# Late loads moved from GpSimd's queue to SyncE's, and half of the spectrum weights loaded early, in an S4 convolution with a one-token expert

## Chip, cores, metric

One core of one Trainium2 chip. The time is device microseconds of a whole execution. A profile is one execution, and its span is some 1.8 us shorter than the time that the same execution is given. Runs are marked fast or slow; a run more than 1.5% above the fastest of its kernel counts as slow, one alone can be of unknown state, and comparisons of times use fast runs.

Engine names in the profile: PE is TensorE's matmuls, PEld its weight loads, DVE is VectorE, ACT ScalarE, POOL GpSimd, SPq SyncE's DMA issues. In the code SP, AC, DV, PO are SyncE, ScalarE, VectorE and GpSimd.

## What is computed

`u` is 2048 x 512 in bf16. The output is `x + s * g`:

```python
xn = layernorm(u)
# S4 convolution by FFT: K[d, l] = Re sum_n C * exp(dt*A*l) * dt*B; y = irfft(rfft(xn, 4096) * rfft(K, 4096))
s  = y + xn * Dskip
# mixture of depths, capacity 1: only the token with the largest r = xn @ w_r goes through the expert
r  = xn @ w_r ; i = argmax(r)
e  = (silu(xn[i] @ w_gate) * (xn[i] @ w_up)) @ w_down * sigmoid(r[i])
g  = silu(xn + scatter(e at i))
out = u + s * g
```

## The kernel before

The FFT is done as matmuls in two steps (F1, then F2T). Between them the data take a round trip through DRAM, which reorders them: AT is stored to `scr_a` and read back as BT. The filter's spectrum K2T is a matmul with the 5.2 MB table W. The product PAB of spectrum and signal goes through the first inverse step (FA), as ZT to `scr_z`, back as DD, and through the last step. The channels come in two halves for AT and BT, and in four parts afterwards.

A program in the kernel lists all operations as numbered nodes, finds their dependences by the memory they touch, and issues them on each engine in the order of fixed lists (`_ORDER`). Each engine issues its list in order, DMAs included, so an entry that waits holds up all behind it: GpSimd stood idle for 42.4 us before WD, and the loads of W came right behind it. The parts that matter here:

```python
_FILL = [(12, 6, 1), (15, 5, 1), ...]       # matmuls whose results nobody reads, by place and PSUM bank; 14 in all
_ORDER = {
    "sync": [..., 188, 198, 193, 203, 392, 391, 393, 394, 390,      # AT stores of half 0, BT reads, AT store of half 1
        385, 380, 375, 420, 430, ...],                              # the other three AT stores, then scr_z stores
    "gpsimd": [
        21, 287, 294, 286, 295, 288, 293, 285, 296, 361, 23, 22, 306, 370, 305, 694, 774, 714, 796,],
    # 21 F2T; 285-288 and 293-296 the expert's gate and up; 361 WD; 22, 23, 305, 306 W by quarters; 370 FA; 694.. XR

o_s = cur[0]                                 # these share AT's memory:
AT = place("AT", [128, 32, 256], BF16)       #   stores 375, 380, 385, 390 each free a quarter of it
cur[0] = o_s
K2T = place("K2T", [128, 2, 2, 2, 256], BF16)        # over the quarter of store 375
PAB = place("PAB", [128, 2, 2, 2, 2, 256], BF16)     # its two buffers: over 380 and 385
ZT = [place(f"ZT{i}", [128, 1024], BF16) for i in range(2)]  # over 390
...
W = place("W", [128, 16, 2, 5, 128], BF16)
FA = place("FA", [128, 16, 3, 128], BF16)
XT = place("XT", [128, 2, 2, 4, 128], BF16, o_w + 25600)     # XT, ERU, ERG, WD lie over W's second half and FA
ERU = place("ERU", [128, 4, 1408], BF16, o_w + 30720)
WD = place("WD", [128, 11, 512], BF16, o_w + 41984)
ERG = place("ERG", [128, 4, 1408], BF16, o_w + 41984)

def wload(k):
    if k is None:
        g.dma(PO, [(FA[:], t_fa.ap()...)])
        return
    g.dma(PO, [(W[:, 4 * k:4 * k + 4], t_w.ap()...)])
...
g.dma(PO, [(WD[:, 0:10, :], ...), (WD[0:96, 10, :], ...)])   # after the gate's matmuls: WD lies on ERG
g.dma(PO, [(XRp[:], ...)])                                    # u again, for the last addition
```

W's first half lies on memory that nothing else uses, so its load depends on nothing.

## Time and profile before

| | before |
|---|---|
| time, median of 4 runs | 192.69 us (192.24 to 193.85) |
| span of the profiled execution | 192.6 us (it took 194.4, marked slow) |
| moved by DMA | 37.18 MB |
| first K2T | 89.94 us |

The profiled execution took longer than all four and is marked slow. The first part of the page gives each engine's busy time, its share of the span and the number of instructions; the third part has the DMA queues with packets, MB and share of the engines' time (q1 is SyncE's queue, q0 GpSimd's). The kernel before:

```profile
PE 144.0 (75%) x2280; PEld 106.9 (55%) x2280; DVE 141.3 (73%) x321; ACT 144.8 (75%) x192; POOL 14.1 (7%) x24
...
q1 hardware_dynamic: 39170, 22.51, 43.1%
q0 software_dynamic: 2464, 14.19, 20.2%
```

No engine is above 75%: the time is in waits.

### The profile page before, as it was taken

The numbers are of one execution on the slowest core, as the hardware profiler recorded it, in microseconds if no ns is written. First come the engines' busy times: TensorE is split into PE (matmuls) and PEld (weight loads), VectorE is DVE, ScalarE is ACT, GpSimd is POOL, SyncE is SP. The second block draws the span as 40 slices with busy tenths as digits, with TensorE's granted clock in tenths as the row PEclk, the third lists the DMA queues.
The fourth block names the chain that finished last, engine by engine and source line by source line (L and its number), as shares of the span: only waits on it lengthen the run. The fifth ranks groups of instructions, "written<-read, shape, count | busy, mean of one in ns | idle before, by whom it ended". The sixth has DMA issues, their size and how long they took to land.

```text
span 192.6 us, 5283 instructions
## 1 busy us (share of the span) xinstructions
PE 144.0 (75%) x2280; PEld 106.9 (55%) x2280; DVE 141.3 (73%) x321; ACT 144.8 (75%) x192; POOL 14.1 (7%) x24
## 2 busy tenths in 40 slices
PE   0213579776699799790999999986999999974580
PEld 0001445663479543370997888863899799931120
DVE  2989899998995799661169999689598375282742
ACT  3998688999977986753799999989787995761031
POOL 0018000000003302000000000020002000400000
PEclk9999999999958969798599999999799999996555
DMA  3899920306696999992002279985000469999984
GB/s 91 249 354 387 394 112 5 109 3 198 180 351 192 242 404 412 429 424 88 0 8 53 54 210 275 235 263 119 2 3 3 112 199 257 191 296 286 216 199 111
DMA packets 41946, 37.18 MB, mean 193 GB/s; under 512 B 26977, under 2 KB 37218, under 8 KB 41026
## 3 DMA queue, kind: packets, MB, share of 16 engines
q1 hardware_dynamic: 39170, 22.51, 43.1%
q0 software_dynamic: 2464, 14.19, 20.2%
q8 instruction: 18, 0.29, 0.6%
q10 hardware_dynamic: 288, 0.13, 0.2%
q14 instruction: 6, 0.05, 0.1%
HBM read 26.34 MB, written 10.49 MB: 191 GB/s over the span
## 4 chain that ended last, share of the span: by engine, by line
PE 37%; DMA 23%; DVE 16%; ACT 15%; SPq 4%; issue 2%; DVEq 0%; ACTq 0%
PE PB L187 36%; DMA scr_a<-AT 15%; ACT AT L758 4%; SPq L210 4%; DVE TT L729 4%; ACT XT L975 4%; DVE ST L821 4%; DMA scr_z<-ZT 3%; DVE PAB L729 3%; DMA X<-in_A_u_dram 3%; DMA DD<-scr_z 3%; DVE GG L729 2%; ACT U L758 2%; ACT SC L758 2%; DVE QQ L729 1%
## 5 line engine op out<-in xcount | busy, mean ns | idle before, releaser
L187 PE MATMUL PB<-KT,W 128*128 128x128 bf16 x640 | 44.4, 232 | 6.1 <-ACT K2T L758 4.5
L187 PEld LDWEIGHTS PB<-KT,W 128*128 128x128 bf16 x640 | 40.1, 105 | 9.2 <-ACT K2T L758 5.0
L729 DVE TENSOR_TENSOR PAB<-U,K2T 128x1024 bf16<-128x1024 bf16 x32 | 21.2, 687 | 23.2 <-ACT K2T L758 23.2
L729 DVE TENSOR_TENSOR TT<-GG,ZB 128x512 bf16<-128x512 bf16 (+2 forms) x64 | 28.0, 468 | 0.5
L758 ACT ACTIVATE K2T<-PB 128x1024 bf16<-128x1024 f32 x16 | 16.5, 1034 | 8.2 <-DMA scr_a<-AT 4.5
L187 PE MATMUL PB<-CA,AD 64*128 64x512 bf16 (+1 forms) x64 | 9.7, 381 | 15.0 <-ACT EE L758 7.2
L729 DVE TENSOR_TENSOR QQ<-QQ,EE 128x2048 bf16<-128x2048 bf16 x16 | 19.5, 1218 | 0.1
L758 ACT ACTIVATE ZT<-PB 128x1024 bf16<-128x1024 f32 x16 | 16.5, 1030 | 3.7 <-PE PB L187 3.7
L758 ACT ACTIVATE KT<-PB 128x640 bf16<-128x640 f32 (+1 forms) x24 | 15.6, 648 | 4.6 <-PE PB L187 4.5
L187 PE MATMUL PB<-PAB,FA 64*128 64x128 bf16 x512 | 17.2, 217 | 0.9 <-DVE PAB L729 0.9
L758 ACT ACTIVATE U<-PB 128x1024 bf16<-128x1024 f32 x16 | 15.9, 1021 | 2.4 <-PE PB L187 2.3
L758 ACT ACTIVATE EE<-PB 128x1024 bf16<-128x1024 f32 x16 | 15.9, 1037 | 1.5 <-PE PB L187 1.4
L758 ACT ACTIVATE AT<-PB 128x1024 bf16<-128x1024 f32 x16 | 16.0, 1076 | 1.3 <-PE PB L187 1.3
L187 PE MATMUL PB<-DD,CB 128*128 128x512 bf16 x32 | 11.8, 503 | 6.1 <-DMA DD<-scr_z 5.8
L187 PEld LDWEIGHTS PB<-PAB,FA 64*128 64x128 bf16 x512 | 14.6, 94 | 3.0 <-DVE PAB L729 1.5
L729 DVE TENSOR_TENSOR GG<-TT 128x512 bf16<-128x512 bf16 (+2 forms) x32 | 15.0, 470 | 0.5
L187 PE MATMUL PB<-XN,CB 128*128 128x256 bf16 (+1 forms) x80 | 13.4, 311 | 1.3 <-ACT AT L758 1.3
L729 DVE TENSOR_TENSOR TF<-PB,XN 128x512 bf16<-128x512 f32 x12 | 8.1, 688 | 8.1 <-PE PB L187 8.1
L187 PEld LDWEIGHTS PB<-CA,AD 64*128 64x128 bf16 x64 | 3.5, 116 | 18.1 <-ACT EE L758 8.6
L187 PE MATMUL PB<-BT,F2T 128*64 128x256 bf16 x128 | 11.0, 299 | 2.5 <-ACT U L758 1.6
L187 PE MATMUL PB<-GG,QQ 128*128 128x80 bf16 x256 | 12.1, 200 | 0.6 <-DVE QQ L729 0.3
L187 PEld LDWEIGHTS PB<-GG,QQ 128*128 128x128 bf16 x256 | 10.4, 98 | 2.1 <-ACT KT L758 0.6
(133 smaller groups left out, 227.0 us busy)
## 6 DMA issues: line engine op xcount, KB each, us to landing
W<-c_w POOLq DMA_DIRECT2D x4, 1280.0 KB, 15.0
scr_a<-AT SPq DMA_DIRECT2D x8, 512.0 KB, 4.4
BT<-scr_a SPq DMA_DIRECT2D x8, 512.0 KB, 5.6
scr_z<-ZT SPq DMA_DIRECT2D x16, 256.0 KB, 4.5
DD<-scr_z SPq DMA_DIRECT2D x6, 512.0 KB, 5.8
XR<-in_A_u_dram POOLq DMA_DIRECT2D x4, 512.0 KB, 6.2
out_dram<-XR SPq DMA_DIRECT2D x8, 256.0 KB, 4.7
X<-in_A_u_dram SPq DMA_DIRECT2D x3, 512.0 KB, 6.0
```

The costliest lines, as they stand in the source:

```text
L187: fns.append(lambda e, o=o, l=l, r=r, st=st, sp=sp, tp=tp: e.matmul(o, lhsT=l, rhs=r, start=st, stop=sp, tile_position=tp, skip_group_chec ...
L210: fns.append(lambda e, dst=dst, src=src: e.dma_start(dst, src))
L729: g.V(lambda e: e.tensor_tensor(out=o, in0=a, in1=b, op=op), [o], [a, b], n, mode)
L758: nd = g.A(lambda e: e.activation(out=o, in_=i, func=func, **kw), [o], ins, n + (110 if "bias" in kw or isinstance(kw.get("scale"), bass.A ...
L821: g.V(lambda e, b=b: e.bn_stats(ST[:, b, :], X0[:, b, :]), [ST[:, b, :]], [X0[:, b, :]], 512)
L975: g.A(lambda e, pv=pv, xt=xt: e.activation(out=xt, in_=pv, func=ACT.Copy), [XT[:, bq % 2]], [PB[:, bank, :]], 1024)
```

## The change

Its intent: the two loads of W's first half, which wait for nothing, go out among the expert's weights; all other late loads leave GpSimd for SyncE; and the order lists of all engines are made anew to suit. The diff, with the lists cut to the places that matter:

```diff
-_FILL = [(12, 6, 1), (15, 5, 1), (43, 4, 2), (49, 4, 2), (69, 4, 1), (72, 4, 3), (73, 4, 3), (206, 2, 1)]
+_FILL = [(12, 6, 2), (17, 5, 1), (33, 1, 1), (35, 1, 1), (43, 4, 1), (44, 4, 3), (49, 4, 2), (50, 4, 2), (65, 6, 1),
+         (66, 6, 3), (70, 4, 3), (71, 4, 1), (73, 4, 2), (76, 4, 1), (205, 2, 1)]
 "sync":
-        ... 188, 198, 193, 203, 392, 391, 393, 394, 390, 385, 380, 375, 420, ...
+        ... 193, 188, 198, 375, 203, 394, 392, 391, 361, 380, 393, 390, 305, 370, 306, 385, 512, 509, 420, ...
 "gpsimd":
-        21, 287, 294, 286, 295, 288, 293, 285, 296, 361, 23, 22, 306, 370, 305, 694, 774, 714, 796,
+        21, 285, 23, 295, 286, 287, 22, 288, 293, 294, 296,
 (the lists of ScalarE, VectorE and TensorE are new too: the same nodes in another order;
  left out as well: three names that nothing reads, and the estimated cost of one node)
-                g.dma(PO, [(FA[:], ...)])
+                g.dma(SP, [(FA[:], ...)])
-            g.dma(PO, [(W[:, tsl], ...)])
+            return g.dma(PO if k < 2 else SP, [(W[:, tsl], ...)])
-            g.dma(PO, [(WD[:, 0:10, :], ...
+            g.dma(SP, [(WD[:, 0:10, :], ...
-            g.dma(PO, [(XRp[:], ...)])
+            g.dma(SP, [(XRp[:], ...)])
```

## The prediction

> **What bounds the kernel now.** I read the page's slices first, then the chain of waits, then the DMA view of the stretch that it points at, then the timelines of the engines there. In the page's slices (each 4.8 us), the rows of TensorE, its clock and the DMA:
>
> ```profile
> PE   0213579776699799790999999986999999974580
> PEclk9999999999958969798599999999799999996555
> DMA  3899920306696999992002279985000469999984
> GB/s 91 249 354 387 394 112 5 109 3 198 180 351 192 242 404 412 429 424 88 0 8 53 54 210 275 235 263 119 2 3 3 112 199 257 191 296 286 216 199 111
> ```
>
> Slices 14 to 17 (67 to 87 us) run at 404 to 429 GB/s, all that this trace ever reaches, and TensorE stands still in slice 18 right behind them. Slices 6 and 8 carry 5 and 3 GB/s: there is an idle DMA system 25 to 45 us earlier. The chain of work that ended last says the same; start, length, what:
>
> ```profile
> 59.43 0.58 SPq L210
> ...
> 61.46 28.40 DMA scr_a<-AT
> ...
> 89.94 1.03 ACT K2T L758
> 90.97 0.05 issue
> 91.02 8.60 PE PB L187 x129
> ```
>
> A 512 KB store of AT, half a spectrum buffer, takes 28.4 us to land, and ScalarE's first K2T waits for it, because K2T lies on AT's memory. The DMA view of 57 to 92 us tells why:
>
> ```profile
> DMA packets 5411, 10.88 MB, mean 311 GB/s; under 512 B 199, under 2 KB 4295, under 8 KB 4766
> q0 software_dynamic: 1104, 8.23, 57.1%
> q1 hardware_dynamic: 4302, 2.58, 26.2%
> ```
>
> GpSimd's queue (q0) has 8.23 MB in 1104 packets, 7.5 KB each; SyncE's (q1) has 2.58 MB in 4302, 0.6 KB each. The timelines of GpSimd, TensorE, ScalarE and VectorE show what loads these are and who pays (the bracket is idle time and its releaser):
>
> ```profile
> 60.85 1.49 POOL L210 DMA_DIRECT2D WD<-in_B_w_down_dram  x2 [42.40 <-PE PB L187]
> 62.34 1.07 POOL L210 DMA_DIRECT2D W<-c_w  x2
> 75.59 0.53 POOL L210 DMA_DIRECT2D FA<-c_fa  x1 [10.91 <-PE PB L187]
> 79.38 1.25 PE L187 MATMUL PB<-KT,W 128*128 128x128 bf16 x10 [1.43 <-DMA W<-c_w]
> 89.94 1.02 ACT L758 ACTIVATE K2T<-PB 128x1024 bf16<-128x1024 f32 x1 [4.52 <-DMA scr_a<-AT]
> 91.02 2.31 PE L187 MATMUL PB<-KT,W 128*128 128x128 bf16 x20 [4.47 <-ACT K2T L758]
> 97.67 0.69 DVE L729 TENSOR_TENSOR PAB<-U,K2T 128x1024 bf16<-128x1024 bf16 x1 [5.38 <-ACT K2T L758]
> ```
>
> The spectrum weights W queue on GpSimd behind WD, which must wait for the expert's gate matmuls (42.4 us of idle before it). So W, WD, FA and the stores of AT all meet in one 27 us stretch.
>
> **What the Trainium skill says.** "DMA: Bandwidth & Descriptors", section "SWDGE vs HWDGE vs iDMA": inside each DMA engine the software and the hardware queues are different ones, and the engine takes turns between them; section "Queues, rings and completion order" puts the turn at a packet. Turns by packet would give q1 0.6 of every 8.1 KB, some 7%, while both have work. The trace agrees in kind: 0.5 MB in 28.4 us is 18 GB/s out of 410. The section "Issuing engines are not separate DMA queues" says that another issuing engine saves only issue time. The trace agrees here too, since one GpSimd issue takes about 0.5 us and GpSimd is 7% busy, so I give the move to SyncE no gain by itself. "TensorE: Matmul & The Clock Gate", section "What's actually happening", states that the clock halves after an idle window of about 3.4 us. The trace: 4.47 us idle before 91.02, clock digit 5 in slice 19, and 20 W matmuls take 2.31 us where the timeline has 1.28 us for the same 20 at 119.9.
>
> **The change, part by part.**
>
> (a) W's first half (two of four 1280 KB loads) goes to GpSimd's second and sixth places after F2T, at about 14 us, among the eight expert loads. It lies in memory that nothing else uses then. Cost: GpSimd then moves 1.05 + 2.82 + 2.62 = 6.5 MB from 13.5 us on; at some 400 GB/s that ends near 30 us. The scr_a stores begin at 33 us, the first expert matmul is at 57. Slices 5 and 6 now have 112 and 5 GB/s. Hidden, cost 0. Gain: 2.62 MB less in the saturated stretch, at 415 GB/s 6.3 us of DMA time.
>
> (b) WD, W's second half, FA and the four XR loads go to SyncE. Big loads and AT's stores then share one queue, and what counts is order. By the listing of the changed program SyncE issues: first AT store (the one K2T lies on), the fourth store of the first half, three BT reads, WD, the second AT store (PAB's first buffer), a BT read, the third one (ZT's memory), W's third quarter, FA, W's last quarter, the last AT store (PAB's second buffer), BT reads. So K2T's store goes first in place of last. FA still waits for the down matmuls (end near 75.0), and the last AT store sits behind FA and W's last quarter: 1.57 + 1.31 + 0.52 MB = 3.4 MB, 8.2 us at 415, plus some 2 us to landing: about 85 us.
>
> Now K2T. ScalarE came free at 85.42 (KT, 84.72 + 0.70). Ahead of that lies TensorE's 1.43 us wait for W, and a wait of 0.27 us for WD, both gone, and the instructions of ScalarE ahead of K2T are the same in number (98). K2T starts at 85.42 - 1.43 - 0.27 = 83.7 in place of 89.94: **6.2 us**. What takes the wait's place: FA lands near 75.0 + 3.8 + 2 = 81, before its first use after PAB (85.5). The second PAB, which needs the 85 us store, comes at about 90. Neither binds.
>
> (c) Between the first and second K2T, 89.94 to 96.61 = 6.67 us, ScalarE waits 0.99 + 0.75 = 1.74 us for TensorE at half clock. Without the 4.47 us of idle the clock should stay up, and TensorE's work from 91.02 to 96.58 shrinks from 5.6 to some 3.3 us. VectorE, which waits 5.38 us for the second K2T and then works without a gap to 117, gets all of it: **1.7 us**.
>
> (d) From 98 to 171 us VectorE, ScalarE and TensorE (33.45 of 33.5 us busy from 134.5 to 168) take turns at full load. Nothing of the change alters this work; it moves earlier as it is: 0.
>
> (e) The tail. XR's loads for parts 1 and 3 now land in 165 to 171 us, and the DMA share is 1.0 up to 183. In the changed order part 3's load goes out before the stores of part 2's last spectrum, 0.5 MB less ahead of the last scr_z store, which took 6.13 us against a median of 4.5. I estimate **0.7 us**.
>
> (f) Costs. 25 filler matmuls in place of 14, seven of them before 57 us; the four more from 57 to 79 at about 0.2 us each are partly in idle time: 0.4. The BT read held behind WD lands at about 62.8 + 1.5 + 2 + DMA backlog = 68 to 69, its matmul was at 69.2: 0.2 on average. Together **-0.6 us**. The start differs in order only (X before AI and STG), where VectorE is bound from 12 us on: 0 with an uncertainty of 1 us.
>
> Sum: 6.2 + 1.7 + 0.7 - 0.6 = 8.0; 192.6 - 8.0 = 184.6, and a little for what I overlooked: **184.8 us**.
>
> **The rivals.**
>
> *SyncE's queue holds things up.* SyncE is in order, and now has waits for matmuls (WD, FA), for VectorE (XR) and for stores to land (XR1) ahead of stores and reads that others need. For it: the last AT store behind FA, and the BT read behind WD. Against it: the waits come within a microsecond or two of when the next entry is ready anyway, and XR1's wait for the out stores ends before the DD read behind it could start. If FA's wait moved out with the down matmuls, the second PAB would wait: 2 to 4 us lost, 187 to 189 us.
>
> *The transfer was hidden anyway.* If the engines from 57 to 90 us were the limit, removing the DMA wait would show another one right behind. ScalarE was free at 85.42 and TensorE at 86.5, so at most 1 or 2 us of the 6.2 could be lost in this way, and the clock's 1.7 might not come: 187 to 188 us.
>
> *The early loads hurt.* W at 14 us competes with the last constants (issued up to 12.7 us, landing some 6 us later) and slows the start, where VectorE is bound. But WD's and the gate's loads compete there already; at most 1 us.
>
> **Range and chances.** The first term is well anchored, the second rests on the clock, the rest is small. All favourable is 182; rival two or one in full is 188. Range 182.0 to 188.3. Over 2% faster means below 188.7: 0.90. Within 2%: 0.09. Slower: 0.01.
>
> **What would show it.** The first K2T near 84 us with no DMA wait; no wait of TensorE for W; about 8 MB between 57 and 92 us with no AT store over 12 us to landing; the clock near full from 84 to 93; PAB's second product near 90; slices 4 to 6 filled with W; everything from gchain's third round on about 8 us earlier. It is wrong if SyncE's queue waits for TensorE while VectorE waits for the last AT store, if K2T finds another wait at the same place, or if the stretch before 57 us grows.

## The result

| | before | after |
|---|---|---|
| time, median of 4 | 192.69 us | 183.07 us (182.97 to 183.65) |
| span of the profile | 192.6 us | 181.3 us |
| first K2T | 89.94 us | 85.48 us |

The ratio is 0.9498, with a 95% interval of 0.9452 to 0.9544: 5% faster. A ratio here and below is the mean time of one kernel's fast runs over that of the other's in the same rounds, so not quite the ratio of the medians. The two profiles differ by 11.3 us, the medians by 9.6, since the profiled execution of before was a slow one of its kind.

The page of the changed kernel, engines, slices (4.5 us each now) and queues:

```profile
PE 139.9 (77%) x2284; PEld 103.3 (57%) x2291; DVE 141.4 (78%) x321; ACT 144.4 (80%) x192; POOL 6.1 (3%) x15
...
PE   0430488977889696969999999996999999975380
...
PEclk9999999997899969987999999999999999999967
DMA  3899999026477899499534256977003799999985
GB/s 97 268 315 376 419 412 364 16 61 174 123 225 225 298 284 354 158 376 314 150 148 99 59 150 139 267 189 144 0 5 82 155 250 271 200 244 258 228 184 116
...
q1 hardware_dynamic: 49266, 30.21, 60.3%
q0 software_dynamic: 1072, 6.49, 8.9%
```

Slices 4 to 6, once 394, 112 and 5 GB/s, now carry W's half at 419, 412 and 364. The hole of TensorE in slice 18 is gone, and so is the clock digit 5 behind it. The engines' busy times are nearly the same: what changed is idle time. The chain of work that ended last (start, length, what) no longer has the store of 28.4 us. Among its DMA pieces the longest is now a read of BT; the store and read at the end are shown with it (the first load of X, 6.12 us, and a store of AT, 4.64 us, are not):

```profile
54.75 6.79 DMA BT<-scr_a
...
85.64 13.70 PE PB L187 x264
...
126.84 32.25 PE PB L187 x630
...
163.68 4.39 DMA scr_z<-ZT
168.08 4.54 DMA DD<-scr_z
```

The timelines at the places that the prediction named, TensorE, ScalarE and VectorE of the changed kernel:

```profile
61.58 0.63 PE L187 MATMUL PB<-BT,F2T 128*64 128x256 bf16 x8 [1.60 <-DMA BT<-scr_a]
85.48 1.02 ACT L760 ACTIVATE K2T<-PB 128x1024 bf16<-128x1024 f32 x1
91.61 0.69 DVE L731 TENSOR_TENSOR PAB<-U,K2T 128x1024 bf16<-128x1024 bf16 x1 [2.17 <-ACT K2T L760]
```

K2T has no wait in front of it, and VectorE's wait for the second K2T is 2.17 us in place of 5.38. But TensorE now waits for BT. The sum, from milestones of ScalarE and VectorE that both timelines show (the first, second and last K2T, the last ZT, the first SV of the last part, the last pair of XR; SV is ScalarE's copy of the last step's result, XR the last addition):

| stretch | before | after | gained |
|---|---|---|---|
| start to first K2T | 89.94 | 85.48 | 4.5 |
| first to second K2T | 6.67 | 5.08 | 1.6 |
| second to last K2T | 71.32 | 68.55 | 2.8 |
| last K2T to last ZT | 3.51 | 3.52 | 0.0 |
| last ZT to first SV of the last part | 13.18 | 11.12 | 2.1 |
| first SV to last XR | 4.18 | 3.76 | 0.4 |

With the 3.8 us from the last pair of XR to the end unchanged, that is the 11.3 us.

### The profile page after: what moved, and what is told of

Same layout as the page of the kernel before. It is cut to its first block, busy times and chain, and to the rows that moved or that the text cites. A ratio compares the mean times of both kernels' runs of the same rounds, so it can differ in the third digit from the quotient of the medians.

```text
span 181.3 us, 5298 instructions
## 1 busy us (share of the span) xinstructions
PE 139.9 (77%) x2284; PEld 103.3 (57%) x2291; DVE 141.4 (78%) x321; ACT 144.4 (80%) x192; POOL 6.1 (3%) x15
## 4 chain that ended last, share of the span: by engine, by line
PE 44%; ACT 20%; DMA 15%; DVE 14%; issue 3%; SPq 3%; DVEq 0%
PE PB L187 43%; DMA BT<-scr_a 4%; ACT XT L975 4%; DVE ST L821 3%; DMA X<-in_A_u_dram 3%; ACT U L760 3%; DVE TT L731 3%; ACT ZT L760 3%; ACT AT L760 3%; DMA scr_a<-AT 3%; SPq L210 3%; DMA DD<-scr_z 3%; DMA scr_z<-ZT 2%; ACT KT L760 2%; ACT QQ L760 2%
## 5 line engine op out<-in xcount | busy, mean ns | idle before, releaser
L187 PE MATMUL PB<-KT,W 128*128 128x128 bf16 x640 | 42.2, 223 | 0.5 <-ACT U L760 0.3
L187 PEld LDWEIGHTS PB<-KT,W 128*128 128x128 bf16 x640 | 37.1, 100 | 4.3 <-ACT K2T L760 1.1
L187 PE MATMUL PB<-DD,CB 128*128 128x512 bf16 x32 | 10.4, 441 | 5.5 <-DMA DD<-scr_z 4.9
L187 PE MATMUL PB<-GG,QQ 128*128 128x80 bf16 x256 | 12.9, 206 | 0.9 <-ACT FT L760 0.3
L187 PE MATMUL PB<-BT,F2T 128*64 128x256 bf16 x128 | 9.9, 279 | 4.2 <-DMA BT<-scr_a 2.9
L187 PEld LDWEIGHTS PB<-GG,QQ 128*128 128x128 bf16 x256 | 11.2, 102 | 1.6 <-ACT KT L760 0.6
L187 PEld LDWEIGHTS PB<-CA,AD 64*128 64x128 bf16 x64 | 3.0, 115 | 14.1 <-DVE AD L744 7.5
L821 DVE BATCH_NORM_STATS2 ST<-X 128x6 f32<-128x512 bf16 x16 | 10.2, 681 | 0.4 <-DMA X<-in_A_u_dram 0.4
```

Of the source, the lines that this page charges most:

```text
L187: fns.append(lambda e, o=o, l=l, r=r, st=st, sp=sp, tp=tp: e.matmul(o, lhsT=l, rhs=r, start=st, stop=sp, tile_position=tp, skip_group_chec ...
L821: g.V(lambda e, b=b: e.bn_stats(ST[:, b, :], X0[:, b, :]), [ST[:, b, :]], [X0[:, b, :]], 512)
```

## The experiments

Three theories of the K2T wait stood beside each other. V, volume: too many bytes between 60 and 90 us. O, order: K2T waits because its own store is issued last of four. Q, queue: the stores' small packets lose their turns to GpSimd's large ones. For each there is one edit of the kernel before that does that alone. The table has all runs, from their profiles (us); the time is the mean of the fast runs. The word behind a label is the state of the profiled run.

| run | first K2T | 1st to 2nd | 2nd to last K2T | ZT to SV | time | ratio to before |
|---|---|---|---|---|---|---|
| before (slow) | 89.94 | 6.67 | 71.32 | 13.18 | | |
| e1 before again (unknown) | 90.46 | 6.57 | 71.06 | 13.20 | | |
| e2 W early | 83.47 | 4.74 | 69.32 | 13.45 | 184.19 | 0.9491 |
| e3 stores in order | 82.09 | 4.75 | 71.45 | 13.10 | 185.51 | 0.9562 |
| e4 late on SyncE (slow) | 86.27 | 4.72 | 70.75 | 13.97 | 185.49, one run | unclear |
| e8 W early and stores | 82.47 | 4.75 | 70.22 | 13.44 | 183.23 | 0.9491 |
| after | 85.48 | 5.08 | 68.55 | 11.12 | 183.19 | 0.9498 |
| e5 after, W late | 84.71 | 5.07 | 68.93 | 12.90 | 184.21 | 0.9555 |
| e6 after, reads first | 81.48 | 5.07 | 68.49 | 11.64 | 181.33 | 0.9450 |
| e7 after, XR on GpSimd | 86.21 | 5.07 | 68.49 | 12.18 | 185.01 | 0.9596 |
| e9 after again (slow) | 86.09 | 5.05 | 68.49 | 11.97 | 182.43 | 0.9449 |
| e10 reads first again | 84.58 | 5.07 | 68.49 | 10.72 | 181.77 | 0.9413 |
| e11 XR on GpSimd again | 83.83 | 5.07 | 68.48 | 11.25 | 182.16 | 0.9440 |
| e12 after, no fillers | 85.44 | 5.07 | 68.64 | 11.21 | 185.20 | 0.9604 |

e1 to e4 were one group on one chip, e5 to e8 another, e9 to e12 a third. Times are to be set against each other within a group; across groups only ratios are, and even these differ by up to 1.7% for one and the same kernel (e7 and e11).

### e1: the kernel before, again

> The kernel before, unchanged, for a profile in the fast state: the first profile of it ran 194.4 us, some 1.7 us above its timed runs. Expected: the same waits at the same places (K2T near 89 us behind a store of AT of over 20 us to landing, TensorE some 1.4 us on W), and a span near 190.7 us. If the span of 192.6 us had been made longer by a lower clock, the difference should sit in stretches of matmuls (134 to 168 us), not in the DMA stretch.

194.58 us, span 192.8. The waits are where they were (K2T at 90.46 behind a store of AT, 6.0 us). The expected span of 190.7 was wrong: on this chip the kernel before took 192.48 to 195.51 us in seven other runs, the longest of them marked slow. So the waits in the profile of before are nothing odd, and the kernel spreads by some 1.6% between executions on one chip.

### e2: W's first half early, nothing else

```diff
-        21, 287, 294, 286, 295, 288, 293, 285, 296, 361, 23, 22, 306, 370, 305, 694, 774, 714, 796,
+        21, 287, 23, 294, 286, 295, 22, 288, 293, 285, 296, 361, 306, 370, 305, 694, 774, 714, 796,
```

> The kernel before with one thing changed: W's first half is loaded at about 14 us, among the expert's weights, by GpSimd as before. Theory V (volume: the stretch from 60 to 90 us has too many bytes, 2.62 MB less frees 6.3 us): K2T near 83.7 us, 185 to 186.5 us in all. Rival O (order: K2T waits because the store it lies on is issued last of four): the store still shares turns with GpSimd's large packets until W's rest, WD and FA are through, FA is issued at 75.6 as before, so K2T moves little, to 87 us or later, and the time stays above 189.

184.19 us against 194.0, ratio 0.9491 (0.9401 to 0.9581). ScalarE's timeline has the first K2T without a wait:

```profile
83.47 1.04 ACT L758 ACTIVATE K2T<-PB 128x1024 bf16<-128x1024 f32 x1
```

The prediction's arithmetic had given 83.7, and its second term, 1.7 us from first to second K2T, came out as 1.93. V's forecast held: two numbers moved in one list bring about as much as the whole change. O's forecast for this run, over 189 us, was wrong.

### e3: AT's stores in the order of their making, nothing else

```diff
-392, 391, 393, 394, 390, 385, 380, 375, 420, 430, ...
+392, 391, 393, 394, 375, 380, 385, 390, 420, 430, ...
```

> The kernel before with one thing changed: the four stores of AT's second half go out in the order in which they are made (the one that K2T lies on first, at about 53 us) in place of last to first. All loads as before. Theory V: the bytes are the same, so some other transfer of the stretch (FA, W, the store under PAB) ends it at about the same 88 to 90 us, and the time stays within 2 us of 192.7. Rival O: K2T starts at 84 to 85.5 us, only the 1.4 us wait for W is left, and the time is 186 to 188.

185.51 us, ratio 0.9562 (0.9493 to 0.9632). ScalarE's timeline and the line on landing times in the view of `scr_a`:

```profile
82.09 1.04 ACT L758 ACTIVATE K2T<-PB 128x1024 bf16<-128x1024 f32 x1
```

```profile
DMA to landing us min/median/max: 3.2/5.7/27.8
```

A store, the last of the four, still crawls for 27.8 us, but it is no longer the one that K2T lies on, and nobody waits. TensorE's wait for W is gone too, so K2T is earlier than O had forecast. O holds as well: with every byte in the same stretch as before, an order of four numbers is enough to free K2T; the time stays 1.3 us above that of e2. V's forecast for this run, within 2 us of before, was wrong.

### e4: the same loads, on SyncE behind the stores

```diff
-"sync":   ... 385, 380, 375, 420, ...
+"sync":   ... 385, 380, 375, 361, 23, 22, 306, 370, 305, 420, ...
-"gpsimd": ... 285, 296, 361, 23, 22, 306, 370, 305, 694, 774, 714, 796,
+"gpsimd": ... 285, 296, 694, 774, 714, 796,
 (and PO becomes SP for WD, W and FA)
```

> The kernel before with one thing changed: WD, W (all of it, late) and FA are issued by SyncE behind the four stores of AT, in the order that GpSimd had; the order of the stores and all of XR as before. Theory Q (queue: the stores crawl because GpSimd's 7.5 KB packets take turns with their 0.6 KB packets): in one queue behind the stores the stores land within 8 us, K2T starts near 85 us, the time is 185.5 to 188. Theory V: the same bytes end at the same time, near 90 us, TensorE waits for W or FA in place of the store, and the time is 191 to 194.

One fast run of 185.49 us and three slow ones (189.03, 189.07, 191.14); the profile is of a slow one, so the size is not settled. What the profile does show is the landing of all `scr_a` transfers:

```profile
DMA to landing us min/median/max: 3.2/4.8/7.3
```

With the same bytes and the same order of stores the longest takes 7.3 us in place of 28.4, and K2T does not wait. The price is that WD is issued behind the stores: TensorE waits 1.8 us for it. By itself e4 does not part the queue from the delay: the loads also went out later (WD at 64.53 us in place of 60.85). The profile of before settles it. From 70 to 85 us its DMA view counts 669 packets on q0 and 669 on q1, one for one, but 5.94 MB against 0.34 MB; in e1 it is 698 against 696. The store that K2T lies on got 5% of the bytes, by turns of one packet. So Q is true of the stores.

### e8: W early and the stores in order

The edits of e2 and e3 together.

> The kernel before with both single edits that worked: W's first half early, and AT's stores in the order of their making. If they remove one and the same wait (K2T behind its store), the second adds nothing to the first: first K2T within 1.5 us of 83.5 us and a time within 1 us of the 184.2 us of W early alone. If they remove different amounts of traffic in turn, the sum would be 8 more: below 181 us.

183.23 us, ratio 0.9491, the same as e2's, though from another chip; a sum of both gains would be 4% lower. The remedies do not add up: they take away one and the same wait.

### e5: the changed kernel with W's half late again

```diff
-"sync":   ... 361, 380, 393, 390, 305, 370, ...
+"sync":   ... 361, 380, 393, 390, 22, 23, 305, 370, ...
-"gpsimd": 21, 285, 23, 295, 286, 287, 22, 288, 293, 294, 296,
+"gpsimd": 21, 285, 295, 286, 287, 288, 293, 294, 296,
 (and all of W on SP)
```

> The changed kernel with one thing undone: W's first half is loaded late again, by SyncE, behind WD, the second store of AT, the last BT read and the third store, and ahead of W's second half. Everything else as changed. If the early load is what carries the gain (theory V), 6.3 us of the 9.6 come back: 187 to 190 us, with K2T or PAB behind a store or TensorE behind W. If the order of the stores is enough by itself (theory O, as the run with the stores in order suggests), the first K2T stays within 2 us of 85.5 us, since its store goes first, and the time is 183 to 185.5.

184.21 us, ratio 0.9555 (0.9503 to 0.9607; the 0.6% to the changed kernel's ratio is across chips and cannot be read), and the first K2T at 84.71. Theory O's forecast held. The changed kernel has two or three remedies for the K2T wait at once, so taking away the one that its description names costs little. A rest of V remains in the view of waits:

```profile
DVE PAB L731 <- DMA scr_a<-AT: 2.6, 1, 2.6
```

VectorE now waits 2.6 us for the last store, the one behind FA.

### e6 and e10: the BT reads first

One part of the prediction that fell short was the stretch up to the first K2T: 85.48 in place of 83.7. SyncE's timeline of the changed kernel:

```profile
53.90 1.28 SPq L210 DMA_DIRECT2D BT<-scr_a  x3
58.85 1.94 SPq L210 DMA_DIRECT2D WD<-in_B_w_down_dram  x2
60.83 0.81 SPq L210 DMA_DIRECT2D scr_a<-AT  x1
61.68 4.58 SPq L210 DMA_DIRECT2D BT<-scr_a  x1
```

BT's reads start 3.1 us later than before (50.77), because a store of the second half stands ahead of the last store they read, and the fourth read stands behind WD. In all TensorE waits 2.9 us for BT (1.0 us in e9, a second profile of the same kernel). The edit:

```diff
-193, 188, 198, 375, 203, 394, 392, 391, 361, 380, 393, 390, 305, ...
+193, 188, 198, 203, 391, 392, 393, 394, 375, 361, 380, 390, 305, ...
```

> The changed kernel with SyncE's order altered: the four BT reads of the first half right behind the stores that they read, ahead of the first AT store of the second half and of WD. In the changed kernel BT's first read is issued 3 us later than before and TensorE waits 1.6 us for it at 61.6, and the first K2T comes at 85.5 in place of the 83.5 of the run with W early alone. If these reads are what delays K2T: K2T at 83 to 84 us and a time 1.5 to 2.5 us below the changed kernel's 183.1. If it is something else (the fillers, the order of the engines), K2T stays near 85.5 and the time within 0.5 us.

> The same kernel as in the run with the reads first before, now beside the changed kernel on one chip. If the late BT reads cost what the first K2T showed (81.5 us against 85.5), the difference is 2 us or more and this is faster than the changed kernel in the mean of the fast runs; if that run of 179.8 us was only a lucky state of the clock, within 1 us.

The reads start at 49.11 and 50.23 us, and the waits for BT are gone in both profiles. e6 took 181.33 us, ratio 0.9450, with no run of the changed kernel beside it. e10 had one: 181.77 against e9's 182.43, 0.4% faster, within the noise. The two profiles of this one kernel have the first K2T at 81.48 and 84.58 us. Their rows of TensorE's clock, e6 first (4.45 us a slice), then e10 (4.5 us a slice):

```profile
PEclk9999999999999999969999999999999999999855
```

```profile
PEclk9999999978999969987999999999999999999968
```

Ahead of the first K2T, e6 has a single low digit (6, the slice from 76 to 80 us); e10 has five (7 and 8 from 36 to 45 us, 6 from 63 to 67.5, 8 and 7 from 76.5 to 85.5), nearly the row of the changed kernel. So the first K2T of one and the same kernel spreads by 3 us from one execution to another, and goes with the clock; an edit worth less than that cannot be read from one profile. The kernel is the fastest and no run of e10 was slow, but that it beats the changed kernel is not shown.

### e7 and e11: XR's loads on GpSimd again

PO for XR in the changed kernel, the four numbers back in GpSimd's list.

> The changed kernel with one thing undone: the four XR loads are issued by GpSimd again, in the order and behind the waits they had. The last store of scr_z took 6.1 us to land before, 6.5 with W early alone, and 4.4 in the changed kernel. If XR's place explains this (term e of the prediction): 6 us again, and a time 1.5 to 2.5 us above the changed kernel. If it is chance or the clock: within 0.6 us of it.

> The changed kernel with XR's four loads on GpSimd again, the same kernel as before, now beside the changed kernel on one chip. If XR's place is worth what the last store's landing showed (6.1 us before, 4.4 changed): 1 to 2 us slower than the changed kernel. If the 2 us between the two medians came from the chip: within 0.6 us.

e7, set against the changed kernel's median from another chip, looked like a loss of 2 us. On one chip, e11 took 182.16 us and e9 182.43, the means of three fast runs each: no difference that these runs can show. Nor does XR's place decide how fast the last `scr_z` store lands: 5.07 us in e7 and 4.61 in e11, where the kernel before had 6.13 and the changed one 4.39. So term (e) of the prediction has the wrong mechanism. e7 was a trap of comparing across groups, and a ratio does not save one from it: for one and the same kernel it was 0.9596 (0.9546 to 0.9646) in e7's group and 0.9440 (0.9356 to 0.9523) in e11's.

### e9 and e12: the changed kernel again, and without fillers

> The changed kernel, unchanged, on the same chip and in the same rounds as the three runs below, which each differ from it in one thing; runs of other rounds were on other chips and their medians cannot be set against each other to a per cent. Expected: 183 us, first K2T at 85 to 86 us, the last scr_z store landing in 4.4 to 5 us.

e9 gave 182.43 us in its fast runs and three slow ones of 184.6 to 185.8.

```diff
-_FILL = [(12, 6, 2), (17, 5, 1), ..., (205, 2, 1)]
+_FILL = []
```

> The changed kernel without any of its 25 filler matmuls, which write nothing that is read. If the fillers hold the clock up (the clock row has 0.7 to 0.9 between 53 and 77 us, and 0.5 in the kernel before): lower clock digits there, and 0.5 to 2 us slower. If they only take TensorE's time ahead of K2T (term f, 0.4 us): 0 to 0.6 us faster.

185.20 us against 182.43: 1.5% slower without matmuls that compute nothing (by the medians of all runs, slow ones too, 185.65 against 183.95, 0.9%). The mean granted clock was 0.91 to 0.93 in its six fast runs, and 0.95 to 0.96 in the three of e9. The clock row of its profile:

```profile
PEclk9999999999675599699999999999999999999955
```

From 45 to 64 us (4.55 us a slice) the digits are 6, 7, 5, 5, where the changed kernel's row has 8, 9, 9, 9 in the same slices. (The expectation misread that row: between 53 and 77 us its lowest digit is 6, not 7.) The first K2T is no later for it (85.44 us), since the changed kernel's row has lows of its own, before and after; the profile is of one execution, and the 1.5% are the timed runs'; where in the kernel they arise is not shown. The fillers earn more than they take.

## Why the prediction was right, and where it was not

The time was forecast as 184.8 us in a range of 182.0 to 188.3 and came out as 183.07. Part of this closeness is luck. The 192.6 us that the prediction started from is the span of a slow execution; that it nearly equals the median time, 192.69, is chance. In gains, 7.8 us were forecast, and 9.6 were measured by the medians, 11.3 by the two profiles. Point by point:

- **(a) W early is hidden.** Right. It fills slices 4 to 6, TensorE's wait for W is gone, and the start is not slower (in e2 the first read of BT is at 51.33 us, in before at 50.77 and in e1 at 51.20). The 2.62 MB did leave the stretch, though from 57 to 92 us there are 9.85 MB, not the forecast 8, since three reads of BT now fall into it; the longest AT store takes 11.1 us. But that this volume is what frees K2T is only one of three sufficient causes: e3 frees it with all the bytes in place.
- **(b) First K2T 6.2 us earlier.** Right in mechanism. Alone (e2) the step is 6.5 us. In the changed kernel it is 4.5, so other parts of the change take some back; which ones is not shown. BT is late (2.9 us of TensorE's waiting, booked as 0.2 in term f): the prediction's own list has one AT store ahead of the store that BT reads, but it booked only the read behind WD. Yet e9 waits only 1.0 us for BT and e10 not at all, and their K2T come at 86.09 and 84.58. At a like mean clock from 40 us on (0.88 to 0.90), the old lists with a remedy (e2, e3, e8) reach K2T at 82.1 to 83.5 us, the new ones (after, e5, e7, e10) at 84.6 to 86.2.
- **The move to SyncE has no gain by itself.** Wrong. This was argued from the time of an issue. e4 shows the other effect: out of GpSimd's queue, and behind the stores, the same loads no longer starve them (7.3 us in place of 28.4), although the prediction had quoted the very rule of turns that makes it so. Its reading of 18 GB/s was also too low: the 512 KB store, a quarter of AT and not half, first stood behind the three others, which had landed at 67.3 us, so its 0.5 MB took some 22.6 us, 23 GB/s.
- **(c) 1.7 us of clock.** Right: 1.6 in the changed kernel, 1.9 in e2 to e4. The mean granted clock from 84 to 93 us is 1.00, and was 0.81. But an idle time as long as those 4.47 us is not needed for a low clock: in before it is also at one half from 69.1, 79.4 and 134.0 us, where no idle piece of TensorE in the 8 us ahead is over 1.8 us.
- **(d) Zero from 98 to 171 us.** Wrong, and the largest miss: 2.8 us. In all six profiles with the order of before, this stretch takes 69.3 to 71.5 us; in all eight with the new lists 68.5 to 68.9. TensorE's timeline of the kernel before has a gap with no releaser in the middle of the second F2T stage, and forty matmuls soon after it, most of them at half the clock:

```profile
129.90 0.84 PE L187 MATMUL PB<-BT,F2T 128*64 128x256 bf16 x11 [0.84 <-issue]
...
134.55 3.74 PE L187 MATMUL PB<-KT,W 128*128 128x128 bf16 x40
```

The changed kernel has no gap there, and the same forty at the full clock:

```profile
126.84 2.41 PE L187 MATMUL PB<-KT,W 128*128 128x128 bf16 x40 [0.29 <-ACT U L760]
```

The gap is at the same instruction in all six profiles with the old order where I looked for it (0.4 to 1.5 us: before, e1, e2, e3, e4, e8) and in none with the new one; the low clock near it is in before and e3 alone. Two more such gaps lie in this stretch, 0.9 us in e3 and 0.4 in e4. Taken off, they leave 68.9 to 69.6 us in e1, e2, e3, e4 and e8, and 70.5 in before, where the low clock cost another 1.3: most of the 2.8 us, if the gaps lie on the path. The view does not name what TensorE waits for, but the packed trace has a trail. The queue q8, marked as instructions, moved 18 pieces of 16 KB, one for about every 256 instructions of TensorE and its weight loads, so I take it for TensorE's own instructions. In all six profiles the gap ends 2.4 to 2.6 us after such a piece started; in the eight with the new lists the piece started 3.3 to 4.4 us ahead of the same matmul, and there is no gap. So TensorE may have run out of fetched instructions there. No run tests this, nor which of the new lists removes it (it isn't W's place, e5, XR's, e11, BT's reads, e10, or the fillers, e12). That stays open.

- **(e) 0.7 us in the tail, by XR's loads being out of the way.** The size was 2.1 us to the first SV, plus 0.4 us from there to the last XR. The place was right, since 1.7 of the 2.1 are the last `scr_z` store (6.13 us before, 4.39 changed), but the mechanism falls with e11: XR is back on GpSimd there, and the store lands in 4.61. Between the last ZT and the first SV the old order takes 13.1 to 14.0 us, the new one 10.7 to 12.9, wherever XR is issued. What is left as a cause is the order of the other transfers on SyncE or another of the new lists; no run takes them apart, so it stays open too.
- **(f) Fillers cost 0.4 us.** Probably wrong in sign: all 25 together save some 2.8 us by the fast runs (e12), 1.7 by the medians of all; the added eleven alone were not run.

So the errors partly cancelled. By the two profiles 3.5 us more were gained than forecast: (d) brought 2.8 us and (e) 1.8 more than booked, (b) 1.7 less, and the 0.6 of (f) does not show as a loss of its own. By the medians it is 1.8 us more, since the profile of before is of a slow run. Of the rivals, the first (SyncE's queue holds things up) came true in part, through BT and not through FA; the other two did not.

## What to carry to other kernels

A buffer that lies on another's memory waits for that one's store, so look at which store is issued last and what lies on it: a list of four numbers was worth nearly as much here as 2.6 MB moved (185.51 against 184.19 us). Small-packet transfers that someone waits for should not stand in one queue while large-packet loads stream through another; put the loads behind them in the same queue, or earlier (here 28.4 us to landing became 7.3, e4, or 15.2, e2). And when one change holds several remedies for one wait, test each alone: each looks like the cause, and undoing one shows almost nothing.

## What the Trainium skill lacked or had wrong

- "DMA: Bandwidth & Descriptors", section "Issuing engines are not separate DMA queues", says that issuing from several engines saves only issue time. No run here tests that for the total bandwidth, but who is served is another matter: with loads of 7.5 KB a packet on GpSimd's queue, a store of 0.6 KB packets on SyncE's took 28.4 us to land; with both on one queue, the loads behind, the longest took 7.3 us (e4). The page states the turns by packet in "Queues, rings and completion order", and the trace agrees (669 packets of each queue from 70 to 85 us), but it does not draw this consequence.
- "TensorE: Matmul & The Clock Gate" advises on idle gaps by the loop's structure or padding; no page has matmuls that compute nothing as a means inside a kernel, beyond warming up a benchmark. Here 25 of them are worth 1.5% (e12, 185.20 against 182.43 us).
